# An adaLN attention and mixer block on one core: wq kept in wo's place, two neighbouring tiles transposed by TensorE, K and V loaded together

## The chip, the cores and the metric

The kernel runs on one core of one Trainium2 chip. The metric is the device time of one execution in microseconds (us). Three runs of the kernel before took 1607.38, 1612.76 and 1612.16 us, median 1612.16.

## The reference

```python
x = A_x                                   # (1, 2048, 640)
sa, ca, ga, sb, cb, gb = rows of (silu(c) @ w_mod)          # six rows of 640
h = layernorm(x) * (1 + ca) + sa
x = x + ga * attention(h, k_cache, v_cache, wq, wo)
h = layernorm(x) * (1 + cb) + sb
x = x + gb * B(h)
return x

def attention(x, k_cache, v_cache, wq, wo):   # 32 heads of 128, 2048 cached keys, no mask
    q = (x @ wq) by heads                     # wq (640, 4096)
    p = softmax(q @ k_cache^T * 128 ** -0.5)
    return (p @ v_cache, heads side by side) @ wo           # wo (4096, 640)

def B(x):                                     # a shifting mixer and an MLP
    hs = shifted(gelu(layernorm(x) @ w1)) @ w2
    x1 = x + hs
    return x1 + gelu(layernorm(x1) @ w3) @ w4
```

All arrays are bf16. Nearly all of the work is the attention: per head 2048 x 2048 scores, their softmax and the product with V.

## The kernel before

The program writes its order by hand. A small planner, `Prog`, keeps one list of operations for each engine in the order of the source, and from the names of what an operation reads (`r`) and writes (`w`) it puts in the semaphore waits. So what stands first in the source is issued first on its engine, and an instruction that waits holds everything behind it on that engine.

**Stages.** A prologue loads x, w_mod, c and the first weights, makes the layer norm, its transpose `hT` and q of head 0. Then comes the attention loop, some 1215 us long. After it, the product with wo, the mixer and the MLP (about 350 us) use the same SBUF areas again: w3, w4 and the output buffers `ob` lie where wo lay.

**The attention loop** (L516) runs over slots s. There are 32 heads of 16 query tiles (128 queries each); in slot s, with h, j = divmod(s, 16), these things happen to tile j of head h:

- `qk` (L279, matmul L286): TensorE makes the scores of the tile against 2048 keys in two halves, in PSUM `Sps`. It reads `QT` (q of the head) and `KTs` (K of the head, transposed; two buffers, heads even and odd).
- L559: DVE copies each half to `negS`, negated and scaled, and takes the minimum (two instructions a tile). L569: GpSimd joins the two minima. L572: ACT takes the exponential into `Pb`, a ring of 8 rows (`RPB`); one row is one tile.
- The tile's probabilities must be transposed for the product with V. For most tiles a DMA does it, issued by SyncE (SP): `transpose` (L220), `dma_start_transpose` at L222, from ring `Pb` into ring `PTs` (12 rows, `RPT`), two neighbouring tiles in one DMA where both go that way. The tiles in `PE_TILES = (3, 10)` are transposed by TensorE instead (`t_piece`, L247, in slots g+3 and g+4, eight key blocks in each) and brought to `PTs` by `t_evac` (L257): on ACT (L262), one half of tile 3 on DVE (L264). Tiles 2 and 11 lose their neighbour and go through DMA alone, so a head has six pairs and two single tiles on SP.
- `pv` (L292, L299): TensorE multiplies a tile with V 11 slots later (`PVD`), 8 slots later near the end. ACT copies the result to `Of` (L550), GpSimd normalizes it (L440, L447) and writes it to a scratch array in DRAM with a DMA from its own queue (L454).
- q of the next head is made in 20 pieces (`q_piece`, L234; 4 column blocks of 5), one in a half slot. They share two PSUM banks (`JB`) with the TensorE transposes, and `taken` (L268) keeps the pieces out of the slots of those. ACT moves each block out (`q_evac`, L244).

**Loads in the loop**, all on SP's queue, in order with the transposes: K of the next head by `load_k` (L203, itself a DMA transpose, from DRAM) at tile 2, wq of the head after next by `load_wq` (L207, 160 KB in rows of 256 bytes, two buffers) at tile 6, V of the next head by `load_v` (L212) at tile 12 (`PVD + 1`). wo (5120 KB) is read once, ahead of the loop, by one DMA (L335); it is used only after the loop.

`Prog` gives each DMA a channel of its own name, and no two transfers of one channel may be in flight. The deadlines of the loads are these: K before the first `qk` of the next head, V before its first `pv` (11 slots later), wq before the first `q_piece`. A row of ring `Pb` is written again 8 tiles later, after its transpose has read it.

Of the kernel before, what the change touches and what calls it, by code (L numbers as in the profile page):

```python
# [115 lines left out]
def bass_adaLN_cond__mha_block_cached__mixer_s_mlp__prompt_kernel(  # L116
# [3 lines left out]
    _, H, SK, DH = A_k_cache.shape  # L120
    FF = B_w3.shape[1]
    assert DH == 128 and D % 128 == 0 and SQ % 512 == 0 and SK == 2048
    KT = D // 128
    NQT = SQ // 128
    NQC = SQ // 512
    NKT = SK // 128
    NFT = (FF + 127) // 128
# [10 lines left out]
    with ExitStack() as es:  # L138
# [11 lines left out]
        if True:  # L150
            with ExitStack() as es1:
                sb1 = lambda name, shape, dt: es1.enter_context(nc.sbuf_tensor(name, shape, dt))
                RPB, RPT = 8, 12
                PVD, PVE = 11, 8
                PE_TILES = (3, 10)
                US = KT * (SQ + 4)
# [18 lines left out]
                Vaug = kv[:, o1:o2].rearrange("p (b k d) -> p b k d", b=2, k=NKT)  # L175
                wq = kv[:, o2:o3].rearrange("p (b k d) -> p b k d", b=2, k=KT)
                QT = kv[:, o3:o3 + 2 * SQ].rearrange("p (b q) -> p b q", b=2)
# [28 lines left out]

                def load_wq(h):  # L207
                    hb = h % 2
                    G.dma("sync", lambda e: e.dma_start(wq[:, hb], A_wq[:, h * 128:(h + 1) * 128].rearrange("(k p) d -> p k d", p=128)),
                          ("wq", hb), w=[("wq", hb)])  # L210

# [22 lines left out]
                def q_piece(h, cc, q):  # L234
                    hb = h % 2
                    jb = bank(("q", h, cc))
                    G.op("tensor", lambda t: t.matmul(JB[jb], wq[:, hb, q, :], hT[:, q, cc * 512:(cc + 1) * 512],  # L237
                                                      start=(q == 0), stop=(q == KT - 1)),
                         r=[("wq", hb), ("hT", cc, q)], w=[("J", jb)])

# [26 lines left out]

                taken = [u for j in PE_TILES for u in range(2 * (j + 3), 2 * (j + 5))]  # L268
                QPIECE = {}
# [56 lines left out]
                for cc in range(2, NQC):  # L326
                    load_x(cc)
                load_wq(0)
                load_k(0)
                load_v(0)  # L330
                load_mod(1, wmodr, 2 * D, 6 * D)
                if H > 1:
                    load_wq(1)
                    load_k(1)
                G.dma("sync", lambda e: e.dma_start(wo[:], A_wo.rearrange("(h p) n -> p h n", p=128)), "wo", w=["wo"])  # L335

# [108 lines left out]
                def norm(gr, z):  # L445
# [5 lines left out]
                    if z < 3:  # L451
# [35 lines left out]
                NEG = [("negS", i) for i in range(3)]  # L487
                KVK = ([("KT", b) for b in range(2)] + [("V", b) for b in range(2)] + [("wq", b) for b in range(2)]
                       + [("QT", b, cc) for b in range(2) for cc in range(NQC)])
# [26 lines left out]
                for s in range(at[-1] + LAG + 1):  # L516
# [10 lines left out]
                    for half in range(2):  # L527
# [10 lines left out]
                        if h + 1 < H and 2 * j + half in QPIECE:  # L538
                            cc, q = QPIECE[2 * j + half]
                            q_piece(h + 1, cc, q)  # L540
                            if q == KT - 1:
                                evacs.append((q_evac, h + 1, cc))
                        for r in range(2):
                            g = s - 3 - r
                            if 0 <= g < NG and is_pe(g):
                                t_piece(g, r, half)
                                if half == 1:
                                    evacs.append((t_evac, g, r))
# [19 lines left out]
                    if s < NG:  # L568
# [6 lines left out]
                        if not is_pe(s):  # L575
                            if s % 2 == 1 and not is_pe(s - 1):
                                transpose(s - 1, 2)
                            elif s % 2 == 1 or is_pe(s + 1):
                                transpose(s, 1)
                        if j == 2 and h >= 1 and h + 1 < H:  # L580
                            load_k(h + 1)
                        if j == 6 and h + 2 < H:
                            load_wq(h + 2)
                        if j == PVD + 1 and h + 1 < H:
                            load_v(h + 1)
                    for g_ in NORMS.get(s, []):
# [37 lines left out]
                def a_pe(j):  # L624
                    b = ybank()
                    pr, z = divmod(j, 2)

                    def f(t):
                        for c0, cw in NC2:
                            for hh in range(H):  # L630
                                ins = t.matmul(YB[b][:, c0:c0 + cw], OTj[pr % 2][:, 2 * hh + z, :], wo[:, hh, c0:c0 + cw],  # L631
                                               start=(hh == 0), stop=(hh == H - 1))
                        return ins
                    G.op("tensor", f, r=[("OT", pr % 2), "wo"], w=[("S", b)])
                    return b
# [37 lines left out]
                for i in range(NQT + 1):  # L673
# [12 lines left out]
                    if 2 <= i:  # L686
                        nrm_of(1, i - 2)
                w3s = B_w3.rearrange("(k p) n -> p k n", p=128)
                G.dma("sync", lambda e: e.dma_start(w3, w3s), "w3", w=["w3", "wo"])
                G.dma("sync", lambda e: e.dma_start(w4[:, 0:NFT - 1, :], B_w4[0:(NFT - 1) * 128, :].rearrange("(f p) n -> p f n", p=128)),  # L690
                      "w4", w=["w4", "wo"])
                G.dma("sync", lambda e: e.dma_start(w4[0:FL, NFT - 1, :], B_w4[(NFT - 1) * 128:FF, :]), "w4b", w=["w4b", "wo"])
                DEL = [1, -1, 2, -2]
# [69 lines left out]
                def e_op(j):  # L763
# [5 lines left out]
                    def f(t):  # L769
                        for c0, cw in NC2:  # L770
# [9 lines left out]
                    G.op("vector", lambda v: v.tensor_add(out=ob[:, u], in0=tmp[:, u], in1=xt[:, j]),  # L780
                         r=[("tmp", u), ("x1", j)], w=[("ob", u)] + (["wo"] if j < 2 else []))
                    G.dma("sync", lambda e: e.dma_start(out2d[j * 128:(j + 1) * 128, :], ob[:, u]), ("out", u), r=[("ob", u)], w=[("o", j)])
# [61 lines left out]
```

## Time and profile before

| | us |
|---|---|
| median of three runs | 1612.16 |
| the profiled execution, its own time | 1604.1 |
| its span (first to last instruction) | 1602.3 |
| busy: PE, DVE, ACT, POOL | 1492.6, 1392.5, 1288.2, 622.8 |
| DVE L559, 1024 instructions, busy | 1177.2 |
| ACT L572, 512 exponentials, busy | 1011.4 |
| median issue to landing: transposes L222, K, V, wq | 7.1, 4.6, 5.2, 3.6 |
| wo, 5120 KB, issue to landing | 16.4 |
| mean granted TensorE clock | 0.993 |

The profile is of one execution, so sums are made against its 1604.1 us; the median of the runs lies 8.1 us higher. A line of a group gives the source line, engine, operation, the tiles written and read, the count, then busy time and mean duration of one, and behind the second bar the idle time of the engine before them with what ended it. An SP line in the timeline gives the start, the length of the issue, and the transfer. PE's busy time counts modelled ends, so it is not a measure of how full TensorE is.

### The profile page before, as it was taken

To read this page: it belongs to the slowest core of one execution; us is meant where nothing else is said; L and a number is where in the kernel's file an instruction comes from. 1 tells how busy PE (TensorE), PEld (TensorE's weight loads), DVE (VectorE), ACT (ScalarE), POOL (GpSimd) and SP (SyncE) were. 2 spreads that over 40 slices of the span, in tenths; PEclk is the share of its full clock that TensorE was granted. 3 is DMA by queue.
4 is the path that set the end of the run, shared out by engine and by line. 5 is a ranking of instruction groups with operands and counts; after the bars stand their busy time and mean duration, and the time that the engine had idled before them with its cause. 6 is when DMAs were issued, how large, how long until landed. Compare 5 with 4: busy or idle time off the path is not lost.

```text
span 1602.3 us, 34804 instructions
## 1 busy us (share of the span) xinstructions
PE 1492.6 (93%) x13978; PEld 963.0 (60%) x14231; DVE 1392.5 (87%) x2460; ACT 1288.2 (80%) x1145; POOL 622.8 (39%) x1394
## 2 busy tenths in 40 slices
PE   5799999999999999999999999999999799999998
PEld 3466666666666666666666666666666555545444
DVE  6999999999999999999999999999999266666424
ACT  4999999999999999999999999999999300055330
POOL 0144444444444444444444444444444423322000
PEclk9999999999999999999999999999999899999999
DMA  9999999999999999999999999999999994530000
GB/s 305 229 230 239 238 243 237 253 241 240 237 237 233 239 237 237 239 239 247 243 250 246 250 239 235 246 228 239 236 244 244 241 196 106 106 111 1 17 17 34
DMA packets 1167730, 333.62 MB, mean 208 GB/s; under 512 B 1148304, under 2 KB 1161552, under 8 KB 1167568
## 3 DMA queue, kind: packets, MB, share of 16 engines
q1 hardware_dynamic: 1161424, 314.59, 98.3%
q0 software_dynamic: 6144, 16.79, 3.3%
q8 instruction: 112, 1.84, 0.5%
q14 instruction: 50, 0.41, 0.1%
HBM read 43.48 MB, written 19.40 MB: 39 GB/s over the span
## 4 chain that ended last, share of the span: by engine, by line
DVE 30%; ACT 24%; PE 20%; DMA 15%; issue 10%; POOL 0%; SPq 0%; ACTq 0%; DVEq 0%
DVE negS L559 27%; ACT ring L572 19%; DMA ring<-ring 13%; PE Sps L631 8%; PE Sps L772 4%; PE Oaug L756 2%; PE QPp L756 2%; ACT ring L262 2%; ACT Of L550 2%; PE Sps L741 1%; ACT kv L244 1%; DMA ring<-in_A_x_dram 1%; DVE ring L364 1%; DMA negS<-o_scratch 1%; PE Sps L286 1%
## 5 line engine op out<-in xcount | busy, mean ns | idle before, releaser
L559 DVE TENSOR_SCALAR_CACHE_REDUCE negS<-Sps 128x1024 f32<-128x1024 f32 x1024 | 1177.2, 1220 | 22.2 <-PE Sps L286 12.5
L572 ACT ACTIVATE ring<-negS,small 128x2048 bf16<-128x2048 f32 x512 | 1011.4, 2029 | 21.9 <-DMA ring<-ring 15.7
L299 PEld LDWEIGHTS PTp<-kv,ring 128*128 128x128 bf16 x8192 | 560.0, 98 | 245.0 <-DMA ring<-ring 6.7
L286 PE MATMUL Sps<-kv 128*128 128x512 bf16 x1949 | 596.3, 383 | 62.8 <-DVE negS L559 42.9
L299 PE MATMUL PTp<-kv,ring 128*128 128x129 bf16 x8192 | 645.6, 221 | 6.5 <-DMA ring<-ring 5.6
L569 POOL TENSOR_SCALAR small<-small 128x1 f32<-128x1 f32 x512 | 145.8, 285 | 621.5 <-DVE negS L559 621.4
L286 PEld LDWEIGHTS Sps<-kv 128*128 128x128 bf16 x2048 | 124.5, 97 | 187.2 <-DVE negS L559 158.0
L447 POOL TENSOR_SCALAR On<-Of,small 128x128 bf16<-128x128 f32 x512 | 189.8, 371 | 13.0
L669 ACT COPY kv<-PTp 128x640 bf16<-128x640 bf16 x32 | 22.0, 692 | 155.0 <-PE PTp L666 154.9
L440 POOL TENSOR_TENSOR small<-Of,small 128x4 f32<-128x4 f32 x128 | 133.2, 1040 | 6.3 <-ACT Of L550 6.2
L454 POOL DMA_DIRECT2D o_scratch<-On x128 | 103.1, 806 | 40.8 <-POOL On L447 37.2
L237 PE MATMUL Oaug<-hTx,kv 128*128 128x512 bf16 x265 | 101.2, 387 | 7.9 <-ACT ring L262 4.2
L550 ACT COPY Of<-PTp 128x259 f32<-128x259 f32 x256 | 99.5, 389 | 10.5 <-PE PTp L299 10.5
L237 PE MATMUL QPp<-hTx,kv 128*128 128x512 bf16 x259 | 97.5, 381 | 2.5 <-ACT hTx L391 1.8
L559 DVE DVE_READ_ACCUMULATOR negS<-Sps 128x1 f32 x1024 | 85.4, 83 | 0.0
L612 POOL TENSOR_SCALAR On<-On 128x1 f32<-128x1 f32 x48 | 24.3, 507 | 152.9 <-DVE On L621 152.9
L639 DVE TENSOR_TENSOR ring<-Sps,mod_bc 128x640 f32<-128x640 f32 x16 | 13.2, 825 | 77.0 <-PE Sps L631 77.0
L631 PE MATMUL Sps<-wo,hTx 128*128 128x128 bf16 (+1 forms) x504 | 71.8, 304 | 5.0 <-DMA hTx<-o_scratch 4.7
L776 DVE TENSOR_TENSOR ring<-Sps,ring 128x640 f32<-128x640 f32 x16 | 13.2, 825 | 66.2 <-PE Sps L772 66.2
L631 PE MATMUL Sps<-wo,negS 128*128 128x128 bf16 (+1 forms) x504 | 69.1, 298 | 1.3 <-DMA negS<-o_scratch 0.9
L262 ACT COPY ring<-Oaug 128x1024 bf16<-128x1024 bf16 x64 | 66.2, 1034 | 0.0
L631 PEld LDWEIGHTS Sps<-wo,hTx 128*128 128x128 bf16 x512 | 40.2, 99 | 36.9 <-DMA hTx<-o_scratch 4.5
(82 smaller groups left out, 1011.2 us busy)
## 6 DMA issues: line engine op xcount, KB each, us to landing
kv<-in_A_v_cache_dram SPq DMA_DIRECT2D x32, 512.0 KB, 5.2
o_scratch<-On POOLq DMA_DIRECT2D x128, 128.0 KB, 4.5
ring<-in_A_x_dram SPq DMA_DIRECT2D x8, 640.0 KB, 4.9
kv<-in_A_wq_dram SPq DMA_DIRECT2D x32, 160.0 KB, 3.6
wo<-in_A_wo_dram SPq DMA_DIRECT2D x1, 5120.0 KB, 16.4
ring<-ring SPq DMA_TRANSPOSE x256, 7.1
ring<-in_w_mod_dram SPq DMA_DIRECT2D x1, 3200.0 KB, 13.6
out_dram<-wo SPq DMA_DIRECT2D x16, 160.0 KB, 1.8
```

Of the source, the lines that this page charges most:

```text
L237: G.op("tensor", lambda t: t.matmul(JB[jb], wq[:, hb, q, :], hT[:, q, cc * 512:(cc + 1) * 512], start=(q == 0), stop=(q == KT - 1)), r=[(" ...
L262: G.op("scalar", lambda a: a.copy(dst, src), r=[("J", jb)], w=[("PT", g % RPT, r)])
L286: ins = t.matmul(Sps[:, col:col + 512], QT[:, hb, j * 128:(j + 1) * 128], KTs[:, hb, col:col + 512], start=True, stop=True)
L299: ins = t.matmul(ob[:, 0:129], PTs[:, b, kt, :], Vaug[:, hb, kt, 0:129], start=(kt == 0), stop=(kt == NKT - 1))
L440: G.op("gpsimd", lambda g: g.tensor_tensor(out=rl[:, 4 * b:4 * b + 4], in0=Of[:].rearrange("p a z d -> p (a z) d")[:, 4 * b:4 * b + 4, 128 ...
L447: G.op("gpsimd", lambda g: g.tensor_scalar(out=On[:, b, z, :], in0=Of[:, 2 * b + z // 2, z % 2, 0:128], scalar1=rl[:, 4 * b + z:4 * b + z ...
L454: G.dma("gpsimd", lambda e: e.dma_start(o_scr[jj // 2:jj // 2 + 2, :, hh].rearrange("a p z d -> p a (z d)"), On[:, b].rearrange("p (a z) d ...
L550: G.op("scalar", lambda a, p=p: a.copy(Of[:, p % 4].rearrange("p z d -> p (z d)")[:, 0:259], PO[:, (p % 2) * 512:(p % 2) * 512 + 259]), r= ...
L559: G.op("vector", lambda v, half=half, s=s, r8=r8: v.tensor_scalar(out=negS[:, s % 3, half * 1024:(half + 1) * 1024], in0=Sps[:, half * 102 ...
L569: G.op("gpsimd", lambda g, r8=r8: g.tensor_scalar(out=nm[:, r8:r8 + 1], in0=nm0[:, r8:r8 + 1], scalar1=nm1[:, r8:r8 + 1], scalar2=None, op ...
L572: G.op("scalar", lambda a, s=s, r8=r8: a.activation(Pb[:, s % RPB, :], negS[:, s % 3, :], ACT.Exp, bias=nm[:, r8:r8 + 1], scale=-1.0), r=[ ...
L631: ins = t.matmul(YB[b][:, c0:c0 + cw], OTj[pr % 2][:, 2 * hh + z, :], wo[:, hh, c0:c0 + cw], start=(hh == 0), stop=(hh == H - 1))
```

## The change

Three things are changed together.

1. wo's SBUF area (40 KB in each partition) is empty until the loop has ended, and wq of all heads is just as large. Now wq of all heads is read into it ahead of the loop, in groups of four heads (`WG = 4`; head 0 alone, heads 1 to 3, then seven groups), in rows of 1 KB; the loads of wq in the loop are gone. When the q pieces of a group of four heads have been made, wo follows into the group's place in one DMA of 640 KB, at tile 11 of heads 3, 7, ..., 31 (`load_wo`). Everything that used the key "wo" now uses the eight keys of the blocks.
2. TensorE transposes tiles 10 and 11 instead of 3 and 10. Tile 10 keeps its lag of 3 slots, tile 11 gets one of 4 (`PE_LAG`), so the pieces stand in slots 13, 14, 15 and the first slot of the next head. DVE moves one half of tile 10. Tiles 2 and 3 now are a pair, and no tile goes through DMA alone: seven pairs a head. The q pieces stand in tiles 1 to 10.
3. K and V of the next head are both issued at tile 11, K first, followed by the block of wo where there is one.

```diff
-                PE_TILES = (3, 10)
+                PE_TILES = (10, 11)
+                PE_LAG = {10: 3, 11: 4}
+                WG = 4
...
-                wq = kv[:, o2:o3].rearrange("p (b k d) -> p b k d", b=2, k=KT)
+                wqg = wo[:].rearrange("p (g h) n -> p g (h n)", h=WG).rearrange("p g (k c) -> p g k c", k=KT)
...
-                def load_wq(h):
-                    hb = h % 2
-                    G.dma("sync", lambda e: e.dma_start(wq[:, hb], A_wq[:, h * 128:(h + 1) * 128].rearrange("(k p) d -> p k d", p=128)),
-                          ("wq", hb), w=[("wq", hb)])
+                def load_wq(h0, h1):
+                    g, c0 = divmod(h0, WG)
+                    G.dma("sync", lambda e: e.dma_start(
+                        wqg[:, g, :, c0 * 128:(c0 + h1 - h0) * 128],
+                        A_wq[:, h0 * 128:h1 * 128].rearrange("(k p) d -> p k d", p=128)),
+                        ("wq", h0), w=[("wq", h) for h in range(h0, h1)])
+
+                def load_wo(g):
+                    G.dma("sync", lambda e: e.dma_start(
+                        wo[:, g * WG:(g + 1) * WG, :],
+                        A_wo[g * WG * 128:(g + 1) * WG * 128, :].rearrange("(h p) n -> p h n", p=128)),
+                        ("wo", g), w=[("wo", g)] + [("wq", h) for h in range(g * WG, (g + 1) * WG)])
...
-                taken = [u for j in PE_TILES for u in range(2 * (j + 3), 2 * (j + 5))]
+                taken = [u % (2 * NQT) for j in PE_TILES for u in range(2 * (j + PE_LAG[j]), 2 * (j + PE_LAG[j] + 2))]
...
-                load_wq(0)
+                load_wq(0, 1)
                 load_k(0)
                 load_v(0)
                 load_mod(1, wmodr, 2 * D, 6 * D)
-                if H > 1:
-                    load_wq(1)
-                    load_k(1)
-                G.dma("sync", lambda e: e.dma_start(wo[:], A_wo.rearrange("(h p) n -> p h n", p=128)), "wo", w=["wo"])
+                load_wq(1, WG)
+                load_k(1)
+                for g in range(1, H // WG):
+                    load_wq(g * WG, (g + 1) * WG)
...
-                        for r in range(2):
-                            g = s - 3 - r
-                            if 0 <= g < NG and is_pe(g):
+                        for r, pt in [(r, pt) for r in range(2) for pt in PE_TILES]:
+                            g = s - PE_LAG[pt] - r
+                            if 0 <= g < NG and g % NQT == pt:
                                 t_piece(g, r, half)
...
-                        if j == 2 and h >= 1 and h + 1 < H:
-                            load_k(h + 1)
-                        if j == 6 and h + 2 < H:
-                            load_wq(h + 2)
-                        if j == PVD + 1 and h + 1 < H:
-                            load_v(h + 1)
+                        if j == PVD:
+                            if 1 <= h < H - 1:
+                                load_k(h + 1)
+                            if h < H - 1:
+                                load_v(h + 1)
+                            if h % WG == WG - 1:
+                                load_wo(h // WG)
```

## The prediction

> **What bounds the kernel now.** I read the page first, then the chain and the waits, then SyncE's timeline.
>
> ```profile
> span 1602.3 us, 34804 instructions
> q1 hardware_dynamic: 1161424, 314.59, 98.3%
> q8 instruction: 112, 1.84, 0.5%
> L559 DVE TENSOR_SCALAR_CACHE_REDUCE negS<-Sps 128x1024 f32<-128x1024 f32 x1024 | 1177.2, 1220 | 22.2 <-PE Sps L286 12.5
> L572 ACT ACTIVATE ring<-negS,small 128x2048 bf16<-128x2048 f32 x512 | 1011.4, 2029 | 21.9 <-DMA ring<-ring 15.7
> ring<-ring SPq DMA_TRANSPOSE x256, 7.1
> ```
>
> DVE runs the two reduces of each query tile and ACT the exponential; in 512 tiles both idle some 22 us. The third full resource is SP's queue q1, which carries all transposes. The chain, in order of time, gives DVE's cadence:
>
> ```profile
> 148.13 5.37 DVE negS L559 x10
> 185.35 5.37 DVE negS L559 x10
> 222.57 5.38 DVE negS L559 x10
> ```
>
> Heads repeat every 37.22 us: 16 tiles of 2.289 and one DVE copy (L264) that adds 0.60. ACT's starts add up to 37.13 a head (16 exponentials 1.905 apart, eight Of copies 0.254, four q evacuations 0.477, three transpose evacuations 0.903). So DVE is the floor.
>
> DVE starts tile 0 at 35.5 and ends its last at 1250.3: 1214.7 us. The floor is 32 x 37.22 = 1191.0, so 23.7 are lost: 4.4 in head 0 (the modulation rows, untouched), 3.3 in head 27, where the windows show a granted clock of 0.96, and 16.0 elsewhere, mostly in heads 10 to 20 (37.4 to 39.1 each). There the waits change:
>
> ```profile
> ACT ring L572 <- DMA ring<-ring: 10.0, 15, 1.2
> DVE negS L559 <- ACT ring L572: 5.3, 9, 1.5
> DVE negS L559 <- PE Sps L286: 3.8, 5, 1.0
> ```
>
> This is from 412 to 830 us; the same view from 77 to 374 us names none of the three. An exponential waits for a slot of the ring of eight Pb rows, which a transpose has not yet read. SyncE's timeline shows why, first unloaded in head 0, then in head 12:
>
> ```profile
> 65.90 6.21 SPq L222 DMA_TRANSPOSE ring<-ring  x2
> ...
> 72.16 0.58 SPq L214 DMA_DIRECT2D kv<-in_A_v_cache_dram  x1
> 75.93 9.00 SPq L222 DMA_TRANSPOSE ring<-ring  x2
> ```
>
> ```profile
> 492.93 0.59 SPq L214 DMA_DIRECT2D kv<-in_A_v_cache_dram  x1
> 493.56 19.24 SPq L222 DMA_TRANSPOSE ring<-ring  x4
> 512.84 2.01 SPq L205 DMA_TRANSPOSE kv<-in_A_k_cache_dram  x1
> 514.89 4.69 SPq L222 DMA_TRANSPOSE ring<-ring  x1
> 519.63 0.59 SPq L209 DMA_DIRECT2D kv<-in_A_wq_dram  x1
> 520.26 10.05 SPq L222 DMA_TRANSPOSE ring<-ring  x2
> ```
>
> Columns: start, length, what. In head 0 SP has gaps; in head 12 none: SP issues without a pause, so start to start is the service time of each item. The waits of L222 that SP's own list puts on ACT (L550, L244) are no cause: they fall inside issues that were already running. Matching issues with exponentials, the transpose of tiles 8 and 9 is through SP 4.05 us after tile 9's exponential in head 0, and 13.1 in head 12 (landing 15.1 after).
>
> Means of the service time over heads 3 to 29: tiles 0/1 4.58, tile 2 alone 2.72, K 2.25, 4/5 4.59, wq 0.64, 6/7 4.84, 8/9 4.63, tile 11 alone 2.25, V 0.63, 12/13 behind V 6.34, 14/15 4.54. The sum is **38.0 us a head against DVE's 37.22**. The ring of eight absorbs the first 9 us of lag (heads 1 to 9); after that the surplus costs time. Part of the 38.0 is stalls: three times a head q1 stands still for 0.75 to 1.8 us just as a packet of q8, the instruction fetch, runs.
>
> **The change part by part.** The forecast is the stream's new sum, and then the slack at its deadlines.
>
> *wq out of the loop*: 0.64 of issue, and the 4.84 behind it becomes 4.58: -0.90 a head.
>
> *Tiles 2 and 3 as a pair instead of tiles 2 and 11 alone*: 2.72 + 2.25 = 4.97 becomes a pair. Loaded pairs take 4.58: -0.39. In head 0 a single took 1.66 and a pair 4.02: there pairing costs 0.70. The stream is loaded, so I stand nearer the first: -0.20. Tiles through DMA stay 14 a head.
>
> *wo in blocks of four heads*: eight reads of 640 KB, one every fourth head, behind V. No such transfer is in the loop before. V (512 KB) costs 0.63 + (6.34 - 4.58) = 2.39; the single wo read of 5120 KB took 16.4, so 2.05 for an eighth. I take 0.63 + 2.05 = 2.7, or 0.67 a head; bounds 0.3 (half of it falls where SP has nothing to do) and 0.9 (V's rate, and the next item held). The Trainium skill (DMA: Bandwidth & Descriptors, Anatomy of one DMA and Bandwidth) gives a DMA, on the GpSimd path, a fixed 2.0 us beside its bytes and would have reads of 1 MiB or more; by it a block is an estimated 3.5 us, 0.2 a head more than I take, which speaks against cutting the one read in eight. The trace disagrees for V: it lands 5.2 us after issue, yet holds the stream up by 2.39.
>
> *K and V together at tile 11*: K 2.25, V 0.63 + 1.76 stay. They move to two tiles in which no DMA transpose comes due: 2 x 2.289 + 0.60 = 5.18 us for 4.64 us of work. V's wait (the last P·V of the head before last, in tile 10) is over by then; behind V on SP stand wo and tiles 12/13, which a late V would hold.
>
> On SP, K passes behind three pairs (4/5 to 8/9), and each of these comes 2.25 earlier for it; POOL's queue, with the o_scratch writes, is passed by nothing.
>
> Sum: 38.0 - 0.90 - 0.20 + 0.67 = **37.6 a head**. Bounds: 37.0 (-0.39, +0.3) and 38.0 (pairing worth nothing, wo 0.9); with the unloaded 0.70 it would be 38.7, but no loaded single came cheaper than half a pair in the mean, so I give that end 1 in 20. 37.6 is still a little over 37.22.
>
> *K's deadline*: now K(h+1) is issued at tile 2 with 30 us to spare. Then it follows tiles 8/9. From DVE's start of tile 9: exponential ended +5.3 (4.8 measured at the least, 0.5 for ACT's lag at that place), pair issued +4.05, K landed +4.7 (its mean): 14.0. QK of the next head (two matmuls, 0.60) must start 0.65 before DVE's tile 16, at 7 x 2.289 + 0.60 - 0.65 = 16.0. **Slack 2 us, where the ring gave 9.** Every us of lag beyond 2 makes PE wait at QK, with P·V, q pieces and TensorE transposes queued behind, then DVE; SP catches up by as much. So the wait settles at the stream's surplus, and the 9 us once absorbed for nothing are gone.
>
> *TensorE and ACT*: the same 16 transposes per tile, evacuations 3 on ACT and 1 on DVE. The clump (tiles 13, 14, 15 and 0 of the next head; DVE takes that of 14) makes ACT's lag (its spacings above, less 2.289 a tile, added up tile by tile) swing by 1.39 over a head, 1.51 before: nothing. The q pieces move to tiles 1 to 10, also 20. If ACT cannot follow, the waits of the weight loads on L262 (9.1 us in the whole span) grow; I allow 0 to +3 in all.
>
> *Start*: wq in eight DMAs instead of wo in one holds SP longer than the 0.58 of L335, perhaps to 45, when the first transpose is due (44.88). The ring hides it; without that cover 2 us. *End*: the last wo block needs no DMA that P·V waits for; nothing.
>
> **The sum.** Surplus 37.6 - 37.22 = 0.36, plus 0.10 because it comes unevenly (wo every fourth head, fetch stalls, and DVE never gives time back): 0.46 x 31 heads = 14 us, against the 16.0 now. Change -2. Profiled execution: 1604.1 (span 1602.3 and 1.8 around it) becomes 1602. The median of the runs is 1612.16, 8.1 above the profiled one, so 1610; as a run with more lag gains a little more by the shorter stream, **1609**.
>
> **Rivals.**
>
> *The stream falls under the cadence (faster).* If a pair saves its 0.39 and half of wo's block falls in the free stretch, the sum is 37.0, no head is surplus, and K's wait is left only behind a stall, some 0.1 to 0.2 a head, 3 to 6 us: 16.0 less these gives -10 to -13, **1600**. For it: q1 moves pairs in 4.02 unloaded. Against: loaded pairs still take 4.58. The Trainium skill (DMA: Bandwidth & Descriptors, Latency and other measured facts) puts transposes at 261 GB/s, an estimated 4.0 us a pair; by that rate the stream would never bind. The trace agrees in head 0 alone.
>
> *K's deadline (slower).* The pairing and wo's bounds go the wrong way, the sum stays at 38.0, and each head waits for K: 0.78 + 0.1 a head, 27 us against 16.0: +11, **1623**. It decides from 37.8 a head up, where (0.58 + 0.1) x 31 = 21 passes the 16.0 by 5. For it: lag of 8 to 10 us already in head 1. Against: wq's 0.90 goes for certain.
>
> *The stream isn't shortened*: if bytes and not items set its pace, wo's 160 KB a head replace wq's 160 KB; ring wait and K wait exchange, **1613**.
>
> **How the numbers follow.** About 0.3% (5 us) can be told from no change, as the runs shown spread by 5.4. Forecast 0.42 (0.12 of it faster, 0.20 within, 0.10 slower), under-cadence 0.26 faster, K's deadline 0.27 slower, bytes 0.05 within. Faster 0.38, same 0.25, slower 0.37. The forecast's own range is 1602 to 1617; for 8 in 10 it reaches over both rivals' values: 1597 to 1626.
>
> **What would show it.** Right: the ACT wait on ring<-ring (15.7) gone; a wait of PE on kv<-in_A_k_cache_dram at L286 in its place, 10 to 16 us, longest after heads 3, 7, 11; wq's SP line out of the loop; heads at 37.5 to 37.8, with none of 37.22 for long. Wrong upward: that K wait over 25 us. Wrong downward: heads of 37.22 throughout and SP with gaps between 8/9 and 12/13. Wrong in kind: L559 or L572 longer, weight loads waiting on L262 above 12 us, or a head 0 longer than 41.6.

## The result: slower, and K is what DVE waits for

After the change the median of four runs is 1633.24 us (1626.67 to 1635.84), before, on the same chip, 1612.46 of four: ratio 1.0128 [1.0087, 1.0168]. The forecast of 1609 and its range up to 1626 were too low. The profiled execution took 1635.84 us, span 1634.0, mean granted clock 0.981 (0.993 before). It lies 31.7 us above the profiled one of before (1604.1), where the medians lie 20.8 apart, so the traces show the loss half again as large as the medians do. The page of the kernel after, the lines that answer to those of before:

```profile
span 1634.0 us, 34765 instructions
...
q1 hardware_dynamic: 1145424, 314.58, 96.8%
...
q8 instruction: 112, 1.84, 0.5%
...
L570 DVE TENSOR_SCALAR_CACHE_REDUCE negS<-Sps 128x1024 f32<-128x1024 f32 x1024 | 1177.8, 1219 | 54.4 <-PE Sps L297 51.9
L583 ACT ACTIVATE ring<-negS,small 128x2048 bf16<-128x2048 f32 x512 | 1023.1, 2020 | 16.6 <-POOL small L580 15.6
...
wo<-in_A_wo_dram SPq DMA_DIRECT2D x8, 640.0 KB, 7.9
...
ring<-ring SPq DMA_TRANSPOSE x224, 7.4
```

DVE's own work is the same to 0.6 us; its idle time rose from 22.2 to 54.4, nearly all put on the scores. ACT's wait on the ring is gone, as forecast. The instruction fetch (q8) is the same; the single transposes are gone from q1 (224 issues for 256), and the eight blocks of wo land 7.9 us after issue. (Lines moved: L559 is now L570, L572 L583, L286 L297, L222 L234.) From the list of waits, with total, count and longest:

```profile
PEld Sps L297 <- DMA kv<-in_A_k_cache_dram: 57.2, 24, 5.6
DVE negS L570 <- PE Sps L297: 51.9, 35, 5.0
PE Sps L297 <- DMA kv<-in_A_k_cache_dram: 51.7, 21, 5.4
```

The loop, from DVE's first tile to its last, grew from 1214.7 to 1247.7 us; what follows it takes 351.0 against 352.0, head 0 41.4 against 41.6. So, in these two traces, all of the loss is in the loop, in heads 1 to 31. The chain of waits shows how one head is lost, at the start of head 5:

```profile
218.07 1.24 DVE negS L570 x3
219.31 0.08 issue
219.39 0.31 POOL small L580
219.70 0.02 issue
219.72 2.00 ACT ring L583
...
224.79 0.76 SPq L234
225.55 0.04 issue
225.59 4.27 DMA kv<-in_A_k_cache_dram
229.86 0.05 issue
229.91 0.87 PE Sps L297 x2
```

SyncE's timeline (start, length, what) has the same K in its second line:

```profile
188.70 36.85 SPq L234 DMA_TRANSPOSE ring<-ring  x7
225.59 1.96 SPq L207 DMA_TRANSPOSE kv<-in_A_k_cache_dram  x1
227.60 0.58 SPq L226 DMA_DIRECT2D kv<-in_A_v_cache_dram  x1
```

SP issued seven transposes in a row from 188.70, without a gap, and came to K at 225.59. Matched with the exponentials, pair 8/9 was through SP 10.6 us after tile 9's exponential, where 4.05 is the unloaded figure. K landed at 229.86, 3.2 us after DVE should have begun head 5.

What came then was not in the prediction. DVE's timeline (start, length, what, idle time before it) at the start of head 9:

```profile
385.91 1.22 DVE L570 TENSOR_SCALAR_CACHE_REDUCE negS<-Sps 128x1024 f32<-128x1024 f32 x1 [4.68 <-PE Sps L297]
...
388.06 1.22 DVE L570 TENSOR_SCALAR_CACHE_REDUCE negS<-Sps 128x1024 f32<-128x1024 f32 x1 [0.92 <-PE Sps L297]
...
390.20 1.23 DVE L570 TENSOR_SCALAR_CACHE_REDUCE negS<-Sps 128x1024 f32<-128x1024 f32 x1 [0.92 <-PE Sps L297]
```

The windows view of the same stretch; behind the length stand the busy times of PE, weight loads, DVE, ACT and POOL, then the granted clock, the DMA share and GB/s:

```profile
385.90:390.20 4.30, 4.08 (x30) 3.20 (x30) 2.46 (x4) 1.22 (x2) 0.64 (x2) 0.50 1.29 264
```

After the wait the granted clock is 0.50 for a while, and DVE waits again for each of the next two half tiles. Start to start, less the 1.1445 of one reduce, DVE loses at the first half tile of heads 1 to 31 **36.4 us** (1.1 before) and at the next five **15.1** (10.5 before, mostly the ring's waits). The 15.1 lie in nine heads (5, 9, 13, 17, 20, 21, 24, 26, 29), the nine in which the records show a stretch of granted clock 0.50 there. Together 51.5; head 0's 4.2 and 1.0 elsewhere make up 56.7, which is 1247.7 less the floor of 1191.0.

### The profile page after: what moved, and what is told of

Read it like the earlier page. It is cut to its first block, busy times and chain, and to the rows that moved or that the text cites. A ratio compares the mean times of both kernels' runs of the same rounds, so it can differ in the third digit from the quotient of the medians.

```text
span 1634.0 us, 34765 instructions
## 1 busy us (share of the span) xinstructions
PE 1498.6 (92%) x13978; PEld 978.8 (60%) x14231; DVE 1393.1 (85%) x2460; ACT 1295.6 (79%) x1145; POOL 622.8 (38%) x1394
## 4 chain that ended last, share of the span: by engine, by line
DVE 36%; PE 25%; ACT 19%; issue 12%; DMA 7%; POOL 1%; SPq 1%; POOLq 0%
DVE negS L570 34%; ACT ring L583 13%; PE Sps L643 7%; DMA kv<-in_A_k_cache_dram 4%; PE Sps L784 4%; PE Sps L297 3%; PE PTp L310 2%; ACT Of L561 2%; PE Oaug L768 2%; PE QPp L768 2%; ACT ring L273 2%; ACT kv L255 1%; PE Sps L753 1%; DMA ring<-in_A_x_dram 1%; DVE ring L375 1%
## 5 line engine op out<-in xcount | busy, mean ns | idle before, releaser
L570 DVE TENSOR_SCALAR_CACHE_REDUCE negS<-Sps 128x1024 f32<-128x1024 f32 x1024 | 1177.8, 1219 | 54.4 <-PE Sps L297 51.9
L583 ACT ACTIVATE ring<-negS,small 128x2048 bf16<-128x2048 f32 x512 | 1023.1, 2020 | 16.6 <-POOL small L580 15.6
L310 PEld LDWEIGHTS PTp<-kv,ring 128*128 128x128 bf16 x8192 | 566.6, 99 | 249.1 <-issue 10.4
L297 PE MATMUL Sps<-kv 128*128 128x512 bf16 x1948 | 600.8, 386 | 92.4 <-DMA kv<-in_A_k_cache_dram 51.7
L310 PE MATMUL PTp<-kv,ring 128*128 128x129 bf16 x8192 | 652.5, 222 | 6.0 <-DMA ring<-ring 4.2
L297 PEld LDWEIGHTS Sps<-kv 128*128 128x128 bf16 x2048 | 137.5, 98 | 208.2 <-DVE negS L570 117.8
L561 ACT COPY Of<-PTp 128x259 f32<-128x259 f32 x256 | 96.3, 376 | 40.2 <-PE PTp L310 40.2
L248 PE MATMUL Oaug<-hTx,wo 128*128 128x512 bf16 x264 | 100.4, 385 | 3.8 <-DVE hTx L407 3.7
L248 PE MATMUL QPp<-hTx,wo 128*128 128x512 bf16 x260 | 98.1, 382 | 2.7 <-ACT hTx L402 2.2
L570 DVE DVE_READ_ACCUMULATOR negS<-Sps 128x1 f32 x1024 | 84.4, 82 | 0.0
```

The source lines that it names most:

```text
L248: G.op("tensor", lambda t: t.matmul(JB[jb], wqg[:, h // WG, q, (h % WG) * 128:(h % WG + 1) * 128], hT[:, q, cc * 512:(cc + 1) * 512], star ...
L297: ins = t.matmul(Sps[:, col:col + 512], QT[:, hb, j * 128:(j + 1) * 128], KTs[:, hb, col:col + 512], start=True, stop=True)
L310: ins = t.matmul(ob[:, 0:129], PTs[:, b, kt, :], Vaug[:, hb, kt, 0:129], start=(kt == 0), stop=(kt == NKT - 1))
L561: G.op("scalar", lambda a, p=p: a.copy(Of[:, p % 4].rearrange("p z d -> p (z d)")[:, 0:259], PO[:, (p % 2) * 512:(p % 2) * 512 + 259]), r= ...
L570: G.op("vector", lambda v, half=half, s=s, r8=r8: v.tensor_scalar(out=negS[:, s % 3, half * 1024:(half + 1) * 1024], in0=Sps[:, half * 102 ...
L583: G.op("scalar", lambda a, s=s, r8=r8: a.activation(Pb[:, s % RPB, :], negS[:, s % 3, :], ACT.Exp, bias=nm[:, r8:r8 + 1], scale=-1.0), r=[ ...
```

## The experiments

The theory after the result was that K's place does it, either because the stream's surplus now shows at K (as forecast, only larger) or because K's deadline loses time that the stream does not need. The rival was that the stream itself got longer (wo's blocks, the pairing). Here "period" is the mean length of heads 3 to 29; SP's share of it is its issues one after the other, about 0.4 to 0.5 of gaps between them, and the rest, in which SP had nothing to issue. A trace is of one execution, and these lie from 8.9 us below the median of their runs (b_tiles) to 5.5 above it (b_vpool); the one of before lies 8 below. Such a difference is 0.26 of a period, so periods that differ by 0.3 can't be told apart.

**K back at tile 2 (a_k2).**

```diff
+                        if j == 2 and 1 <= h < H - 1:
+                            load_k(h + 1)
                         if j == PVD:
-                            if 1 <= h < H - 1:
-                                load_k(h + 1)
```

> The changed kernel with one edit: K of the next head is issued at tile 2 again, not at tile 11; V and the wo blocks stay at tile 11, tiles 10 and 11 stay with TensorE, wq stays ahead of the loop. Deadline theory (the loss is K's place: its landing comes too late for QK, and after each such wait SyncE runs dry): PE's wait on kv<-in_A_k_cache_dram (51.7 us) goes to under 3 us, SyncE is never idle, and the time falls by 20 to 30 us to 1603-1613, at or a little under the kernel before. Stream theory (the loss is a longer DMA stream, by the wo blocks and the pairs, wherever K stands): the wait turns back into ACT's wait for ring<-ring, and the time stays at 1622 or more.

Measured: 1610.25, ratio to before 0.9992 [0.9972, 1.0012]. The wait on K is gone from the list of waits, and this stands in its place:

```profile
ACT ring L583 <- DMA ring<-ring: 23.1, 23, 2.4
DVE negS L570 <- ACT ring L583: 12.4, 20, 1.2
```

The whole loss hangs on K's place. The rest of the change, with K early, is worth nothing either way: the period is 38.13 us, SP idle for 0.02 of it, so nothing shows that the stream has become shorter than in the kernel before (37.83, in an execution 8 us under its median).

**No wo in the loop (a_nowo, and a_k2_nowo with K at tile 2 as well).** In neither is wo ever read, so the product with wo uses what wq left in its place. The edit of the first:

```diff
-                            if h % WG == WG - 1:
-                                load_wo(h // WG)
```

> The changed kernel with the eight wo blocks left out of the loop (wo is never read, so the product with wo uses what wq left there). It prices the blocks. Heads 4, 8, 12, ..., which follow a block, took 41.2 on average against 38.4 of the others. Deadline theory: those heads fall to the 38.4 of the others, 7 x 2.8 = 20 us less, and K's wait stays in all heads, some 20 to 30 us of it: 1611-1616. Stream theory: the blocks are the whole surplus, K's wait falls under 8 us, and the time goes to 1600 or less.

> K at tile 2 and no wo block in the loop at all (the product with wo uses what wq left there); tiles 10 and 11, wq ahead, V at tile 11 as in the change. It prices the wo blocks where no deadline is tight. With K at tile 11 they cost 1633.2 - 1601.2 = 32 us, 4.0 a block, while SyncE's service times hold only about 2.9 a block. Deadline theory: with K early the ring of eight takes up the lag, so a block costs at most its 2.9 and part of that is absorbed: 1610 less 10 to 18, so 1592-1600, with heads at 37.2 for most of the run and ACT's wait for ring<-ring under 10 us. Rival (a block costs 4 us wherever K stands): 1585 or less.

Measured: 1601.19, ratio 0.9928 [0.9902, 0.9954], and 1594.88, ratio 0.9893 [0.9848, 0.9937]. The first, which lies between the two expectations (1611 to 1616, and 1600 or less), still waits for K in its list of waits:

```profile
PE Sps L297 <- DMA kv<-in_A_k_cache_dram: 30.2, 23, 2.7
```

With K late the eight blocks cost 1633.24 - 1601.19 = 32 us, 4.0 each; with K early 1610.25 - 1594.88 = 15 us, 1.9 each (by the intervals of the ratios, each to about 1 us). The same transfer costs about twice as much where a deadline stands close behind it. It is also the first sign that K's deadline loses time by itself: a_nowo's period is 37.76, though SP issues for only 36.94, 37.3 with the gaps, and has nothing to issue for 0.45.

**Tiles 10 and 11 alone, on the kernel before (b_tiles).**

```diff
-                PE_TILES = (3, 10)
+                PE_TILES = (10, 11)
+                PE_LAG = {10: 3, 11: 4}
```

> The kernel before with the tiles alone: TensorE transposes tiles 10 and 11 (lags 3 and 4) instead of 3 and 10; K at tile 2, wq at tile 6, V at tile 12 as before. Deadline theory: no deadline is touched, so within 5 us of 1612; by the sum of the prediction 0.2 us a head less of stream, -3 to -6. Stream theory, clumped work: 8 us or more above 1612, with ACT waiting longer for ring<-ring or DVE for ACT.

Measured: 1614.37, ratio 1.0009 [0.9986, 1.0031]; period 37.95 against 37.83. Seven pairs instead of six pairs and two singles save SP nothing that can be seen.

**wq ahead and wo in blocks, on the kernel before (b_wq).** The loads of the change, but tiles 3 and 10, K at tile 2, V at tile 12, the block at tile 6:

```diff
-                        if j == 6 and h + 2 < H:
-                            load_wq(h + 2)
+                        if j == 6 and h % WG == WG - 1:
+                            load_wo(h // WG)
```

> wq alone: wq of all heads ahead of the loop in wo's place and wo in blocks of four heads, here at tile 6 of heads 3, 7, ...; TensorE keeps tiles 3 and 10, K stays at tile 2, V at tile 12. By the terms of the prediction (wq 0.90 saved, blocks 0.67 paid) the stream is 0.23 a head shorter: about 1606. By the stream as measured since (a_k2: 38.1 a head, no shorter than before) the saving is eaten by the blocks: 1609-1616. A rival that blames the reading of wq in wo's place (longer start, q pieces): 1620 or more, with head 0 longer than 41.6.

Measured: 1612.7, ratio 1.0017 [0.9999, 1.0034]; period 37.80. What wq frees, wo takes.

**K alone at tile 11, on the kernel before (b_k11).**

```diff
-                        if j == 2 and h >= 1 and h + 1 < H:
+                        if j == PVD and h >= 1 and h + 1 < H:
                             load_k(h + 1)
```

> The kernel before with K alone moved, from tile 2 to tile 11 (there behind the single transpose of tile 11); all else as before. Deadline theory: K's wait appears at QK in nearly every head and costs as much as in the changed kernel or more, since here K also stands behind tile 11 and wq stays in the loop: 1625-1645, PE waiting for K 35 to 70 us. Stream theory: the stream is the same, so within 5 us of 1612.

Measured: 1659.1, ratio 1.0288 [1.0252, 1.0324], worse than was expected and worse than the whole change. From its list of waits:

```profile
DVE negS L559 <- PE Sps L286: 74.1, 62, 3.7
...
PE Sps L286 <- DMA kv<-in_A_k_cache_dram: 60.1, 28, 3.9
```

28 short waits, one in nearly every head. SP is far from full here: it is busy for 36.70 of a period of 39.59 and has nothing to issue for 2.38. Pair 8/9 is through SP 4.7 us after its exponential in the mean, close to unloaded, and K is late nevertheless. So this is a chain of latencies, not a surplus. Tile 11 still goes by DMA here, and K stands behind that single transpose, 1.75 to 3.7 us more, beyond the slack. The run therefore shows what a deadline does that is missed in every head; it is not the change's own place for K, where tile 11 isn't on SP.

**K at tile 8 (a_k8).** As a_k2, with `j == 8`, so K passes ahead of pair 8/9.

> The changed kernel with K issued at tile 8, one pair of transposes (8/9) earlier than in the change; all else as in the change. K's slack grows by one service time, from 2 us to about 6.7. Deadline theory: heads without a wo block behind them stop waiting (their lag at K was 2 to 4 us over the slack of 2), heads behind a block, whose transposes land 12 to 14 us after their exponentials, still wait 1 to 2 us; PE's wait for K falls from 51.7 to 5-15 us, the time from 1633 to 1611-1619. Rival (any K that stands behind the pairs pays the same, the place within the head does not matter): 1628 or more.

Measured: 1617.12, ratio 1.0037 [1.0014, 1.006]. From its list of waits:

```profile
PE Sps L297 <- DMA kv<-in_A_k_cache_dram: 21.5, 14, 3.1
...
ACT ring L583 <- DMA ring<-ring: 16.8, 17, 4.5
```

The time is as expected; it lies 6.9 us above a_k2, where the change lies 23.0 above it. Fewer heads wait for K, but their waits add up to 21.5 us, more than the 5 to 15 expected, and now the ring's wait is there too.

**Blocks where they do least harm (a_late).** K at tile 2; the first two blocks at tile 11 of heads 7 and 15, the third at tile 2 of head 31, the other five behind its last transposes; the product with wo waits block by block.

```diff
+                WOAT = {(7, PVD): (0,), (15, PVD): (1,), (H - 1, 2): (2,), (H - 1, NQT - 1): (3, 4, 5, 6, 7)}
...
+                        for g in WOAT.get((h, j), ()):
+                            load_wo(g)
```

> A version meant to beat both: K at tile 2, and the wo blocks out of the loop but for three (heads 7, 15 and 31); the other five are issued behind the last transposes, where SyncE's queue is otherwise nearly empty; the product with wo waits block by block. Deadline theory with the stream sum: about 37.4 a head, so the loop loses 3 to 8 us where it now loses 16; behind the loop the five blocks (2 us each) delay the first products by 0 to 7 us. 1597-1606. Rival (the late blocks hold the transposed scratch array back by their whole length): 1608-1614.

Measured: 1608.27, ratio 0.9991 [0.9971, 1.0012]. The loop shortens to 1213.1, but what follows it grows by 7.4 to 359.4; the largest wait there, from the list of waits:

```profile
PE Sps L645 <- DMA hTx<-o_scratch: 12.5, 1, 12.5
```

It was 4.7 in the kernel before: the read of the attention's result queues behind the five blocks. So the rival of the expectation holds; the time lies above the 1597 to 1606, and is no faster than before.

**V off SP: in eight pieces on GpSimd's queue (b_vpool on the kernel before; a_k2_pool and a_pool on the change, with wo there too, K at tiles 2 and 11).** They ask whether SP's stream is limited by issue or by bytes.

```diff
-                    G.dma("sync", lambda e: e.dma_start(Vaug[:, hb, :, 0:128], A_v_cache[0, h].rearrange("(t p) d -> p t d", p=128)),
-                          ("v", hb), w=[("V", hb)])
+                        G.dma("gpsimd", lambda e: e.dma_start(
+                            Vaug[:, hb, i * VP:(i + 1) * VP, 0:128],
+                            A_v_cache[0, h, i * VP * 128:(i + 1) * VP * 128].rearrange("(t p) d -> p t d", p=128)),
+                            ("v", hb, i), w=[("V", hb, i)])
...
+                        v_pieces(h, j)
+                        if j == 10 and h % WG == WG - 1:
+                            load_wo(h // WG)
```

> The kernel before with V taken from SyncE's queue: eight pieces of 64 KB from GpSimd's queue (tiles 12 to 15, and 1, 3, 5, 7 of the next head); all else as before. It asks what sets the length of the stream. If SyncE's issues one after the other set it (service theory), the stream loses 0.63 and the 1.8 behind V, 2.4 a head of 37.9, DVE's cadence is the bound, the ring waits go, and the loop comes near its floor: 1594-1600. If the DMA engines' bytes set it (byte theory), the same bytes come by another queue and the transposes get slower by as much: 1608-1615. GpSimd gets 8 x 0.8 = 6.4 us a head more; if its minimum (needed by the exponential) comes late through that, DVE waits for ACT instead, and the time is above 1615.

> As the last one, with K at tile 2: wq ahead, tiles 10 and 11, V and wo on GpSimd's queue. Service theory: SyncE's stream is about 35.5 a head, no deadline is tight, DVE is the bound in all heads: 1589-1596, the fastest of all, K's and the ring's waits under 3 us. Byte theory: as a_k2, 1605-1612.

> The changed kernel, K still at tile 11, but V (eight pieces) and the wo blocks on GpSimd's queue. SyncE is left with seven pairs and K, some 35.5 us a head. Deadline theory in the form that the wait is only the stream's surplus (the step of the prediction): no surplus, so no wait for K, 1592-1598. Deadline theory in the form of a chain (exponential of tile 9, pair 8/9, K, QK, with 2 us of slack, so that every stall in that chain is lost though SyncE has time to spare elsewhere): PE still waits 5 to 15 us for K, with short drops of the granted clock behind the longer waits: 1598-1610.

Measured, against 1617.59 of before on that chip: b_vpool 1613.32, ratio 0.997 [0.994, 0.9999]; a_k2_pool 1614.09, 0.9973 [0.9947, 0.9999]; a_pool 1653.89, 1.0223 [1.0185, 1.0261]. In the first SP has V no more, and still it is never idle (0.02): what V left is filled by slower transposes (start to start, pair 8/9 5.15 instead of 4.63, tile 11 alone 3.28 instead of 2.25). Its period of 38.33 is from an execution 14.7 us longer than the one of before, on another chip, and shows no more than that. By the medians on one chip V's leaving is worth 4.3 us, where a limit of SP's issue would give 12 or more; that fits one pace of bytes for both queues. Against the 1612 for which the expectations were written, the service theory's ranges end at 0.993 and 0.990; both runs lie above, close to the byte theory's, which begin at 0.998 and 0.996. The gains, 0.3%, are at the edge of what can be told. a_pool goes against both expectations; from its list of waits:

```profile
PE Sps L313 <- DMA kv<-in_A_k_cache_dram: 67.3, 26, 7.5
```

SP is idle 3.11 us a head, and K is later than ever: the block, issued at tile 10, now moves at the same time as pair 8/9, whose issue takes 7.32 us in the heads with a block and 4.76 in the others, and then K (4.7 to 8.4 us to land), so the long waits come before heads 4, 8, 16, 20, 28, at once and not a head later.

**Keeping TensorE busy through the wait (a_warm, a_warm1).** Fourteen matmuls of data at hand go ahead of the first QK of a head: in heads 4, 8, ..., 28 in the first run, one head too early, and in 5, 9, ..., 29, where the waits are, in the second.

```diff
+                    if s < NG and j == 0 and h > 1 and h % WG == 1:
+                        def warm(t, hb=h % 2):
+                            for i in range(14):
+                                ins = t.matmul(Sps[:, (i % 2) * 512:(i % 2) * 512 + 512], QT[:, hb, 0:128],
+                                               KTs[:, 1 - hb, 0:512], start=True, stop=True)
```

> The changed kernel with 14 extra matmuls (QK of the head before, written into Sps and overwritten; some 3 us of TensorE work) ahead of the first QK of heads 4, 8, ..., 28, the heads that wait longest for K. It separates the wait from what follows it. In the changed kernel DVE loses 36.4 us in the first half tile of the heads (K's wait) and 15.1 in the next five half tiles, and in the windows the granted clock drops to 0.96-0.97 in those heads. Clock theory (TensorE idle for over about 2 us gets half the clock for 3.4 to 6.8 us afterwards, and its QK then holds DVE): with TensorE busy through most of the wait the loss in the next five half tiles of these heads (about 8 us in all seven) falls under 3 us, the waits stay, and the time falls by 3 to 8 us to 1625-1630. Rival (work that heaped up behind the waiting QK, P·V and transposes, holds DVE afterwards, whatever the clock): the loss stays or grows, as 3 us of work more stand in the queue: 1633-1640.

> As a_warm, with the 14 extra matmuls one head later, ahead of the first QK of heads 5, 9, ..., 29: these are the heads that wait 2.5 to 5 us for K in the changed kernel (K issued behind a wo block's lag, one head on); in a_warm the matmuls stood a head too early and made pauses of their own. Clock theory: the waits for K of these seven heads stay at 2.5 to 5 us, but the loss in the five half tiles behind them falls from 10.3 to under 3 us; 7 to 9 us less than the change on the same chip, a ratio to the kernel before of about 1.007 to 1.009. Rival (heaped-up work): the loss behind the waits stays at 8 or more and the ratio at 1.012 or more.

Measured: 1622.45, ratio 1.0045 [1.0026, 1.0063], and 1625.64, 1.0058 [1.0038, 1.0077]; the change itself has 1.0128 [1.0087, 1.0168]. DVE's timeline of the second at the start of head 9:

```profile
390.37 1.22 DVE L577 TENSOR_SCALAR_CACHE_REDUCE negS<-Sps 128x1024 f32<-128x1024 f32 x1 [4.13 <-PE Sps L297]
391.52 0.08 DVE L577 DVE_READ_ACCUMULATOR negS<-Sps 128x1 f32 x1
391.52 1.22 DVE L577 TENSOR_SCALAR_CACHE_REDUCE negS<-Sps 128x1024 f32<-128x1024 f32 x1
```

And its windows there:

```profile
386.00:390.30 4.30, 2.92 (x16) 1.22 (x15) 0.24 (x2) 2.97 (x3) 1.67 (x3) 1.00 1.19 214
390.30:394.60 4.30, 4.30 (x51) 3.16 (x49) 4.23 (x7) 2.64 (x3) 0.64 (x2) 1.00 1.33 171
```

The wait is nearly as long as it was (4.13 for 4.68), the clock stays at 1.00 and nothing is lost behind it. Over the span, the first half tiles lose 40.2 (36.4 in the change) and the five behind them 4.8 instead of 15.1; in the seven heads with the extra work 3.2 instead of 10.3, nearly all of it in heads 5 and 25, where the wait was longest and the clock fell all the same. So at least 10 of the 15.1 were the clock's, and filling the gap with useless work gets these back; the ratio is a little better than the 1.007 to 1.009 expected. In the first run the seven artificial pauses of 2.66 (18.6 us) let SP catch up, so that the long waits at heads 9, 13 and on shrink: the first half tiles lose 12.3 us beside these pauses and the halves behind 3.1. It comes out close to the second by another road, and is no clean test of the clock.

## Why the prediction was wrong

**What held.** DVE's cadence and the floor; the ring's wait replaced by a wait of PE on K; no cost at the start, the end, for TensorE's transposes or ACT's order (the weight loads of the q pieces, which waited 9.1 us on TensorE's evacuations before, do so no more; those of P·V do once, for 1.9). "Slack 2 us" held: K lands in time where pair 8/9 is through SP at most 15.95 - 4.8 - 4.8 = 6.3 us after its exponential (DVE's start of tile 9 to the due time, less the exponential's lag, less K's landing), against 4.05 unloaded. It was the rival "K's deadline", priced at 1623 and given 0.27, that came true, and at 1633 even that was priced too low.

**The step that failed: "So the wait settles at the stream's surplus".** It took the deadline for a second ring, only smaller, in which SP ends every head as far behind as the slack allows and never stops. It does stop. After the change SP has nothing to issue for 0.89 us a head (0.03 before), 2.38 in b_k11, 3.11 in a_pool. Pair 8/9's lag is 4.1 to 8.3 us in most heads, 9.6 to 11.1 in heads 4, 8, 12, 16 and 28, and 8.8 and 8.0 in heads 20 and 24; these seven are the ones behind a block. What goes past 6.3 is lost at once, before head 5, 9, 13, and on; DVE, delayed, then gives SP time, SP catches up, and has nothing to do, since it can't transpose tiles that are not yet made. SyncE's timeline has such a stop late in head 9, which has no block (V, then pair 12/13 and what follows):

```profile
421.25 0.58 SPq L226 DMA_DIRECT2D kv<-in_A_v_cache_dram  x1
423.22 14.78 SPq L234 DMA_TRANSPOSE ring<-ring  x3
```

Of the 24 us that SP so lost in heads 3 to 29, near 11 stand at this one place, between V and pair 12/13, in eight heads where pair 8/9 was 4.1 to 6.4 us behind; in a_nowo it is 10 of 12. It is the stretch of tiles 10 and 11, which no longer go through DMA. The prediction put K and V there as 4.64 us of work for 5.18 us of time; an SP that is punctual enough for K is through with both before tiles 12 and 13 are made. Most of the rest stands at the start of heads 9, 13, 17 and 29, which DVE began 3.9 to 5.1 us late. The ring carried a late spell over into many heads, K's deadline charges each one. The period went up by 1.24 us against before (37.83 to 39.07): 0.31 more of issue, 0.07 of gaps and **0.86 in which SP had nothing to do**. I had 0.10 a head for unevenness; that is the term that the 0.89 replaces, 0.79 more a head, 24 us in 31 heads. The stream's own sum, too low by 0.5 a head (below), is worth another 15 in the prediction's formula. Together that is more than the 34 us by which the profiled execution lies above its forecast of 1602, so the parts are good to some 5 us; both terms failed, and the idle one is the larger.

**Never priced: the clock.** 15.1 us behind the waits, 0.49 a head; a_warm1 shows the cause. It isn't to be added to the idle time above: DVE's late tiles are what SP then waits for. The window of 0.96 in head 27 was in the prediction as a loss of 3.3 us, and I didn't ask what a longer idle stretch of TensorE would do to it.

**Terms that were mis-sized.** The stream, summed as in the prediction from the mean service time of each item, is 38.1 a head after the change, not 37.6. Taking out wq and pairing tiles 2 and 3 was to give -1.10 from 38.0; the same sum is 37.3 in a_nowo, -0.7, and 37.6 in a_k2_nowo, -0.4. Of it pairing gives nothing (b_tiles has 38.0). A sum that depends on K's place isn't the sum of fixed prices that the prediction took it for. wo's blocks give 37.69 - 36.94 = +0.75 a head in SP's busy time, 3.0 a block, for 2.7 forecast, within its bounds; the run's time charges 1.9 or 4.0 for one, by the place of K. The Trainium skill (DMA: Bandwidth & Descriptors, Anatomy of one DMA) gave an estimated 3.5 for a block; the 3.0 of the trace lies between that and mine. The sum lies just outside its bounds of 37.0 to 38.0.

**A sign that was off by a head.** I looked for the longest waits "after heads 3, 7, 11". K of head 4 stands ahead of the block on SP; the block delays what follows, up to K of head 5. In a_pool, where the block doesn't queue behind K, the waits do come before heads 4, 8, 16.

**Also seen.** The rival "bytes set the pace" was given 0.05 and a time, 1613, that is near that of every kernel with K early (a_k2 1610, b_wq 1613, b_tiles 1614). The pool runs speak for its mechanism too: copies that leave SP's queue slow the transposes left on it. So does b_tiles, which has fewer items and the same bytes and gains nothing, and a_k2_nowo, which has fewer bytes and does. What I can't say is what sets this pace. And no version that does the whole work beats the kernel before by more than can be told: a_late and a_k2 stand at 0.999, with 1 within both intervals, b_vpool and a_k2_pool at 0.997.

## What to carry to other kernels

When a load is moved closer to its use, count how much late service the old place absorbed and whether lateness is averaged there or charged head by head: with a slack of 2 us, bursts of 3 us on the same queue were paid, although the queue was idle afterwards. Price a shared queue's transfer by where it stands, not only by its length; here one block cost 1.9 or 4.0 us. And when a change makes TensorE wait for more than about 2 us, add the slow clock behind the wait, here 0.9 to 2.3 us each time, to the price of the wait.

## What the hardware showed

**The clock drops after short idle stretches.** In after, a_nowo, b_k11 and a_warm1 every idle stretch of PE above 2.4 us in the loop was followed by a granted clock of 0.50, none under 1.95 us was, and between the two some were. Other runs widen this zone at both ends: in a_k8 one of 2.44 us was not followed by it, in a_pool one of 1.92 was, and in the kernel before the clock fell in head 27 (the window of 0.96) 1.8 us behind an idle stretch of 1.43. PE's ends are modelled, so these lengths are rough. The low clock lasted 3.41 or 6.83 us each time. The Trainium skill (TensorE: Matmul & The Clock Gate, HAM oscillation) has half rate after idle gaps over about 3.4 us, judged in windows of that length. The half rate agrees with the traces, and so does the 3.4 as the length of a low stretch; as a threshold it doesn't, for drops follow gaps of 2 to 2.4 us.

**Queues share a pace.** Within one trace, a_pool, the issue of pair 8/9 took 7.32 us in the seven heads in which a block of wo moved beside it on GpSimd's queue, and 4.76 in the other heads: 2.6 us more, near the 3.0 that a block takes of SP's time on SP's own queue. In a_k2_pool the block meets pairs 4/5 and 6/7, and 6/7 takes 6.90 against 4.77. In these runs a copy put on another queue took nearly the same time from the transposes.
